# Attention with mean-pooled queries and a two-layer MLP on one core: unsplit float32 for the first five head pairs, and keys that are kept in DRAM

## The chip, the cores and the metric

One core of a Trainium2 chip runs one program. The metric is the device time of one execution in microseconds (us). The kernel before was run three times: median 1096.42 us, from 1094.15 to 1097.43.

## The reference

```python
def _attn_ref(q, k, v):                       # 4 batches, 8 heads, 1152 keys, 64 per head
    q_pool = q.reshape(B, H, S // 2, 2, D).mean(axis=3)
    scores = scale * np.matmul(q_pool, k.transpose(0, 1, 3, 2))
    scores = scores - np.max(scores, axis=-1, keepdims=True)
    attn = np.exp(scores)
    attn = attn / (np.sum(attn, axis=-1, keepdims=True) + 1e-09)
    return np.matmul(attn, v)
def _moe_ref(x, w_in, w_out):                 # x: 2304 x 512, 512 -> 2048 -> 512
    h = x @ w_in
    g = np.maximum(0.01 * h, h)
    return g @ w_out
```

The attention output, with the heads side by side, is x. All inputs are float32, but for w_in and w_out, which are float64 and are converted in the kernel.

## The kernel before, in words

**Split numbers.** Each operand of a large matmul is written as hi + lo. ScalarE (ACT) copies it from PSUM into the type float32r, which gives hi; VectorE (DVE) subtracts that from the original, which gives lo. The keys of a head are stacked in `kk` (hi in one half of the 128 partitions, lo in the other), the queries are doubled in `qq`, so two matmuls per 384 columns (lines 393, 394 and 397, 398) give all four products. In P·V the values hi and lo stand side by side in `vv` as 128 output columns, and the two parts of `et` are streamed through them one after the other (line 477, 18 matmuls per unit); `norm` adds the two halves of the result.

**Units.** A unit is one head of one batch and one group of its 576 pooled query rows: group 0 has 256 rows in 2 tiles, group 1 has 320 rows in 3 tiles. Batches 0, 1 and 2 (`HALF_FIRST`) are passed twice: first group 0 of all eight heads, then group 1 of all eight; batch 3 is passed once, both groups of a head after each other. That makes 64 units: 0 to 7 are group 0 of batch 0, 8 to 15 its group 1, 16 to 31 are batch 1, 32 to 47 batch 2, 48 to 63 batch 3. Heads are taken in pairs (segments `sg`); a pair's keys are loaded, transposed (`k_tr`, line 311, nine transposes), and split (`k_hi`, `k_lo`, line 326) anew in each pass, so batches 0 to 2 do it twice.

**A unit's steps.** `load_q`, `q_sum` (GpSimd, POOL), `q_tr`, `q_hi`, `q_lo` (line 357); for each tile `qk`, `vmax` (line 406, the maximum from PSUM on DVE), `exp` (line 420, ACT); then `rsum` (lines 429, 433: sum and reciprocal on DVE), `r_tr` (line 438: the reciprocals transposed, so that they lie along the columns), `tr` (line 457: 18 or 27 transposes of the exponentials), `e_hi` (ACT) and `e_lo` (line 466, DVE), `pvm` (line 477), `norm` (ACT copy, DVE line 489, POOL line 492), and `x_out` (line 497), which writes a piece of x to DRAM. `tr` of a unit comes after its `r_tr`, by an order constraint.

**The MLP** goes over nine blocks of 256 rows of x: `x_load` (line 571), `l1` (line 593, 192 matmuls of 256 columns per block), `post`, `l2` (lines 615 to 617, 96 matmuls of 512 columns per block). Block 0 needs units 0 to 7, blocks 6, 7 and 8 need batch 3. The 32 weight tiles are converted from float64 along the way (`w_load`, `w_f32`, `w_hi`, `w_lo`: lines 520 to 545, seven passes of 512 columns each over ACT, DVE and POOL).

**Order.** A planner (`Scheduler`) places every step on its engine at build time: of the steps that can start, by the costs that it assumes, it takes the one with the lowest `prio`, which is counted in tiles with offsets (`AHEAD`, `SOONER`, `TR`, `PV`, `WIN`, `WOUT`). Each engine then runs its list in that order. SyncE (SP) issues all DMAs, from one list. The eight PSUM banks are handed out by tags: `s` (one slot of two banks, scores of 768 columns), `s2` (one bank, the other 384), `t` (three banks, all transposes), `o` (P·V), `ml` (one bank, the MLP).

Of the kernel before, what the change touches and what calls it, by code (L numbers as in the profile page):

```python
# [150 lines left out]
def tile_pooled_attention_moe(  # L151
# [52 lines left out]
    NU = len(units)  # L204
    visits = {}
# [54 lines left out]
    stats = [sb.tile([128, 12], F32, name=f"stat{i}") for i in range(3)]  # L260
    xd = [dram.tile([DM, SP], F32, name=f"xd{b}") for b in range(B)]
# [11 lines left out]
    tags["ml"] = [(None, 0, slots("bank", (6,))), (tail, 0, slots("bank", (0,), (1,), (2,), (3,), (4,), (7,)))]  # L273
# [31 lines left out]
    def k_tr(sg, gi, e, i, *heads):  # L305
        for j, x in enumerate(heads):
            kk[2 * sg + j] = new("kk", x)
# [19 lines left out]

    qn, qs, qps, qq = {}, {}, {}, {}
# [16 lines left out]
    def q_tr(u, e, i, s):  # L345
        p, t = QG[units[u][2]]
        qq[u] = new("qq", s)[:, :, :p * t]
# [13 lines left out]
    vn, vv = {}, {}  # L361

# [49 lines left out]
    def exp(u, j, part, e, i=None, s=None):  # L412
# [5 lines left out]
        d = ex[u, j][:n, 2 * CW:] if part else ex[u, j][:n, :2 * CW].rearrange("p (c k) -> p c k", c=2)  # L418
# [40 lines left out]
    def e_hi(u, x, e, i):  # L459
        et[u, x] = new("et", i)  # L460
# [9 lines left out]
    def pvm(u, x, e, i=None):  # L470
# [4 lines left out]
        for a, t in enumerate(kts(u)[x]):  # L475
            for y in range(2):
# [5 lines left out]
    def norm(u, step, e, i):  # L482
# [152 lines left out]

    def trs(*rows):
# [17 lines left out]
    for u in range(NU):  # L654
# [8 lines left out]
        if u == us[0]:  # L663
            if j == 0:
                for part in range(1 if sg else len(KLOAD)):
                    before = ("load_k", sg, part - 1) if part else ("load_k", sg - 1, 0 if sg > 1 else len(KLOAD) - 1) if sg else None
                    step(load_k, sg, part, prio=pr - 4 + 0.01 * part - (0 if sg else 50), **sp(1, 0.59e6 if sg else 0.15e6), order=[before],
                         takes=[("kn", [("k_tr", sg, NCH - 1)])] if part == 0 else [])
                heads = [2 * sg, 2 * sg + 1]
                for gi in range(NCH):  # L670
                    hold = [(f, sg, gi, x) for f in ("k_hi", "k_lo") for x in range(len(KPART[gi]))]
                    need = [0] if sg else [[0], [1, 2], [3]][gi]
                    step(k_tr, sg, gi, prio=pr + 0.1 * gi, eng=trs(128, 128, 128),
                         deps=[("load_k", sg, x) for x in need] + [("k_tr", sg, gi - 1) if gi else ("k_tr", sg - 1, NCH - 1) if sg else None],
                         takes=[("t", hold)] + ([("kk", [("qk", us_of[x][-1], len(tiles_of(us_of[x][-1])) - 1, 1)]) for x in heads] if gi == 0 else []))
# [3 lines left out]
            step(load_v, hd, prio=pr + 2, **sp(1, 0.3e6), order=[("load_v", hd - 1) if hd else None], takes=[("vr", [("v_lo", hd)])])  # L679
            step(v_hi, hd, prio=pr + 5, eng={"ACT": act(576), "DVE": dve(576, 2)}, deps=[("load_v", hd)], order=[("v_hi", hd - 1) if hd else None], takes=[("vv", [("pvm", us[-1], len(kts(us[-1])) - 1)])])  # L680
            step(v_lo, hd, prio=pr + 5, eng={"POOL": gp(576)}, deps=[("v_hi", hd)])
# [24 lines left out]
        step(r_tr, u, prio=p0 - 1, eng=trs(*[x[1] for x in tiles_of(u)]), deps=[("rsum", u, 1)], takes=[("t", [("r_cp", u)])])  # L706
        step(r_cp, u, prio=p0 - 1, eng={"ACT": act(w, True)}, deps=[("r_tr", u)], takes=[("rb", [("norm", u, 2)])])
# [96 lines left out]
```

## Time and profile before

| | us |
|---|---|
| median of three runs | 1096.42 |
| the profiled execution | 1097.69 |
| its span, first to last instruction | 1095.9 |
| PE (TensorE) busy | 997.1 (91%) |
| DVE / ACT / POOL busy | 775.8 / 689.6 / 406.2 |
| 16 DMA engines, mean busy share | 44% |

The span is what the rows of the trace add up to; the profiled execution is 1.8 us longer, and 1.3 us above the median. Busy time of PE overstates its work, since a matmul's record includes its way through the array, while the next one already follows: what a matmul costs in a row of matmuls is the distance between two starts.

### The profile page before, as it was taken

To read this page: it belongs to the slowest core of one execution; us is meant where nothing else is said; L and a number is where in the kernel's file an instruction comes from. 1 tells how busy PE (TensorE), PEld (TensorE's weight loads), DVE (VectorE), ACT (ScalarE), POOL (GpSimd) and SP (SyncE) were. 2 spreads that over 40 slices of the span, in tenths; PEclk is the share of its full clock that TensorE was granted. 3 is DMA by queue.
4 is the path that set the end of the run, shared out by engine and by line. 5 is a ranking of instruction groups with operands and counts; after the bars stand their busy time and mean duration, and the time that the engine had idled before them with its cause. 6 is when DMAs were issued, how large, how long until landed. Compare 5 with 4: busy or idle time off the path is not lost.

```text
span 1095.9 us, 19300 instructions
## 1 busy us (share of the span) xinstructions
PE 997.1 (91%) x6748; PEld 906.3 (83%) x6748; DVE 775.8 (71%) x1625; ACT 689.6 (63%) x1693; POOL 406.2 (37%) x402
## 2 busy tenths in 40 slices
PE   5666788988999989999999999999999999799998
PEld 4555677787898979989899989988999888789896
DVE  7898889997788787777788788776778666411110
ACT  6777877877677666667677667776667665311110
POOL 5666557654233243222434242223222231133220
PEclk8788989999999999999999999999999999899999
DMA  8866546252264353524444433524243130286640
GB/s 263 283 213 214 179 141 232 84 210 90 73 203 143 103 161 100 170 79 150 144 157 134 136 129 116 182 66 162 76 136 105 30 125 25 63 293 231 191 164 29
DMA packets 83953, 158.55 MB, mean 145 GB/s; under 512 B 8592, under 2 KB 44944, under 8 KB 83856
## 3 DMA queue, kind: packets, MB, share of 16 engines
q1 hardware_dynamic: 83856, 157.32, 43.8%
q8 instruction: 53, 0.87, 0.3%
q14 instruction: 44, 0.36, 0.1%
HBM read 139.46 MB, written 17.83 MB: 144 GB/s over the span
## 4 chain that ended last, share of the span: by engine, by line
PE 68%; DVE 18%; issue 5%; DMA 4%; ACT 2%; POOL 2%; SPq 0%; DVEq 0%; POOLq 0%; ACTq 0%
PE banks L593 15%; PE banks L457 11%; PE banks L477 11%; PE banks L615 5%; PE banks L617 5%; PE banks L616 5%; DVE mx L406 5%; PE banks L393 4%; PE banks L394 4%; DVE kk L326 3%; DVE et L466 2%; PE banks L397 2%; PE banks L311 2%; PE banks L398 2%; DVE raw L529 2%
## 5 line engine op out<-in xcount | busy, mean ns | idle before, releaser
L466 DVE TENSOR_TENSOR et<-banks,et 128x320 fp32r<-128x320 f32 (+2 forms) x448 | 233.5, 536 | 70.3 <-ACT et L194 66.8
L194 ACT CAST et<-banks 128x320 fp32r<-128x320 f32 (+2 forms) x448 | 201.2, 470 | 120.5 <-PE banks L477 67.0
L406 DVE TENSOR_REDUCE mx<-banks 128x1 f32<-128x768 f32 (+2 forms) x320 | 234.2, 751 | 60.0 <-PE banks L394 49.9
L420 ACT ACTIVATE e<-banks,mx 128x768 f32<-128x768 f32 (+2 forms) x320 | 238.2, 745 | 56.6 <-DVE mx L410 49.8
L477 PE MATMUL banks<-et,vv 128*128 128x320 f32 (+1 forms) x1152 | 245.9, 323 | 5.8 <-DVE mx L410 4.1
L593 PE MATMUL banks<-xb,ws 128*128 128x256 f32 x1728 | 243.9, 286 | 7.8 <-ACT g L601 2.2
L457 PE MATMUL banks<-ident,e 128*128 128x128 f32 (+2 forms) x1440 | 219.2, 275 | 33.7 <-DVE et L466 14.5
L593 PEld LDWEIGHTS banks<-xb,ws 128*128 128x128 f32 x1728 | 224.2, 190 | 15.5 <-ACT g L601 4.8
L457 PEld LDWEIGHTS banks<-ident,e 128*128 128x128 f32 (+2 forms) x1440 | 174.9, 147 | 61.9 <-DVE et L466 21.6
L477 PEld LDWEIGHTS banks<-et,vv 128*128 128x128 f32 x1152 | 171.0, 194 | 10.8 <-DVE mx L410 5.0
L343 POOL TENSOR_TENSOR qs<-qn 80x256 f32<-80x256 f32 (+1 forms) x128 | 78.5, 633 | 195.8 <-PE banks L351 134.0
L606 POOL TENSOR_TENSOR gg<-g,gg 128x512 fp32r<-128x512 f32 x62 | 80.2, 1294 | 178.4 <-DVE gg L194 146.2
L393 PE MATMUL banks<-kk,qq 128*128 128x384 f32 (+2 forms) x320 | 118.1, 369 | 9.3 <-ACT e L420 9.1
L373 POOL TENSOR_TENSOR vv<-vr,vv 128x576 fp32r<-128x576 f32 x56 | 80.2, 1432 | 97.1 <-DVE vv L194 87.7
L394 PE MATMUL banks<-kk,qq 128*128 128x384 f32 (+2 forms) x320 | 111.4, 348 | 1.0 <-DVE qq L357 1.0
L326 DVE TENSOR_TENSOR kk<-banks,kk 64x384 fp32r<-64x384 f32 (+1 forms) x224 | 98.9, 454 | 14.2 <-ACT kk L194 10.0
L601 ACT ACTIVATE g<-banks 128x512 f32<-128x512 f32 x72 | 43.0, 597 | 102.2 <-PE banks L593 101.5
L615 PE MATMUL banks<-wo,gg 128*128 128x512 f32 x248 | 101.9, 411 | 0.9 <-ACT g L601 0.7
L194 ACT CAST kk<-banks 64x384 fp32r<-64x384 f32 (+1 forms) x224 | 83.9, 392 | 23.6 <-PE banks L311 13.7
L617 PE MATMUL banks<-wo,gg 128*128 128x512 f32 x248 | 97.6, 394 | 0.0
L616 PE MATMUL banks<-wo,gg 128*128 128x512 f32 x248 | 97.4, 393 | 0.0
L492 POOL TENSOR_TENSOR xo<-x,rb 64x256 f32<-64x256 f32 (+1 forms) x64 | 53.1, 829 | 71.4 <-DVE x L489 67.3
(60 smaller groups left out, 1275.1 us busy)
## 6 DMA issues: line engine op xcount, KB each, us to landing
ws<-wd SPq DMA_DIRECT2D x144, 512.0 KB, 4.3
vr<-in_v_dram SPq DMA_DIRECT2D x56, 288.0 KB, 3.4
kn<-in_k_dram SPq DMA_DIRECT2D x27, 576.0 KB, 3.9
raw<-in_moe_w_in_dram SPq DMA_DIRECT2D x16, 512.0 KB, 5.4
wd<-ws SPq DMA_DIRECT2D x16, 512.0 KB, 4.1
raw<-in_moe_w_out_dram SPq DMA_DIRECT2D x16, 512.0 KB, 5.0
qn<-in_q_dram SPq DMA_DIRECT2D x32, 160.0 KB, 2.4
out_dram<-raw SPq DMA_DIRECT2D x18, 256.0 KB, 2.0
```

What stands on the lines that cost most here:

```text
L194: ENG[e].copy(out=out, in_=in_) if e == "ACT" else ENG[e].tensor_copy(out=out, in_=in_)
L393: nc.tensor.matmul(p[:, c], lhsT=hi, rhs=key[:, c * CW:(c + 1) * CW], start=True, stop=False)
L394: nc.tensor.matmul(p[:, c], lhsT=lo, rhs=key[:, c * CW:(c + 1) * CW], start=False, stop=True)
L406: nc.vector.tensor_reduce(out=m[:, part:part + 1], in_=sps[u, j, part], axis=(AX.XY, AX.X)[part], op=ALU.max)
L420: nc.scalar.activation(out=d, in_=sps.pop((u, j, part)), func=AF.Exp, bias=mxs[u, j][:n, 2:3], accum_out=st[u][:n, c:c + 1])
L457: nc.tensor.transpose(p[:, a * w + o:a * w + o + n], ex[u, j][:n, t * 128:(t + 1) * 128], ident[:n, :n])
L466: nc.vector.tensor_tensor(out=et[u, x][:, 1, :w], in0=tps.pop((u, x))[:, :w], in1=f32(et[u, x])[:, 0, :w], op=ALU.subtract)
L477: nc.tensor.matmul(p, lhsT=vv[vis_of[u]][:, korder[vis_of[u] % 2][t], :], rhs=et[u, x][:, y, a * w:(a + 1) * w], start=(t == 0 and y == 0) ...
L593: nc.tensor.matmul(p, lhsT=wst[i, f][:, a, c, :], rhs=xx[i][:, x, c, :], start=(n == 0), stop=(n == 3 * KC - 1))
L615: nc.tensor.matmul(p, lhsT=gh, rhs=wo[f][:, 0], start=(f == hf * FH), stop=False)
L616: nc.tensor.matmul(p, lhsT=gh, rhs=wo[f][:, 1], start=False, stop=False)
L617: nc.tensor.matmul(p, lhsT=gl, rhs=wo[f][:, 0], start=False, stop=(f == hf * FH + FH - 1))
```

## The change

The first five head pairs (`PLAIN = 5`: units 0 to 9) stay in unsplit float32. Their keys are copied once (`k_cp`, ACT or DVE), with one pair's two heads in one `kk` tile; `qk` is three float32 matmuls per tile that contract over 64 partitions (512 + 512 columns from the two halves of the partitions, then 128); `e_hi` is one copy on either engine, with no `e_lo`; `pvm` is nine float32 matmuls of 64 output columns; V is loaded straight into `vv`; `norm_plain` is one DVE multiply. The split keys of the eight pairs of batches 1 and 2 are written to DRAM in the first pass (`k_save`) and read back in the second (`k_back`), which drops their second `k_tr`, `k_hi` and `k_lo`. `r_tr` gets a later priority, loses the order constraint and produces 64 partitions instead of 128. Until the exponential of unit 7's second tile, `s` has two slots (banks 0, 1 and 6, 7), `t` has two banks and `ml` has none. The planner's offsets change.

```diff
+PLAIN = 5
+KEEP = True
+RT = 2.5
+EARLY = 7
-AHEAD = 3.0
-SOONER = 4.0
-TR, SPLIT, PV = 1.5, 1.0, 2.0
+AHEAD = 4.0
+SOONER = 6.0
+TR, SPLIT, PV = 2.0, 1.0, 3.0
-WIN = (-2.0, 0.8)
-WOUT = (20.0, 1.0)
+WIN = (0.0, 1.0)
+WOUT = (16.0, 0.6)
...
+    kept = {sg: first_seg[bh] for sg, bh in enumerate(seg_bh) if KEEP and PLAIN <= first_seg[bh] < sg}
...
-    tags["s"] = [(None, 0, slots("bank", (0, 1)))]
+    early = ("exp", EARLY, 1, 0)
+    tags["s"] = [(None, 0, slots("bank", (0, 1))), (None, early, slots("bank", (6, 7)))]
-    tags["t"] = [(None, 0, slots("bank", (3,), (4,), (7,)))]
+    tags["t"] = [(None, 0, slots("bank", (3,), (4,))), (early, 0, slots("bank", (7,)))]
...
+    def k_cp(sg, gi, e):
+        copy(e, kk[2 * sg][:, gi * CW:(gi + 1) * CW], kps.pop((sg, gi)))
+    def k_save(hd, e):
+        nc.sync.dma_start(out=kd[hd], in_=f32(kk[hd]))
+    def k_back(hd, e, i):
+        kk[hd] = new("kk", i)
+        nc.sync.dma_start(out=f32(kk[hd]), in_=kd[2 * kept[hd // 2] + hd % 2])
...
+        if plain(u):
+            head = units[u][4]
+            p = new(("s", "s2")[part], i)
+            p = sps[u, j, part] = p[:n, :128] if part else p[:n]
+            for c in [2] if part else [0, 1]:
+                half, first, m = ((head, 4 + 4 * head, 1) if part else ((head + c) % 2, (4 + c) * head, 4))
+                nc.tensor.matmul(
+                    p if part else p[:, c], lhsT=qq[u][64 * half:64 * half + 64, 0, o:o + n],
+                    rhs=kk[2 * units[u][3]][64 * half:64 * half + 64, 128 * first:128 * (first + m)], start=True, stop=True,
+                )
+            return
...
-            nc.tensor.transpose(p[:, o:o + n], st[u][:n, 8 + j:9 + j].to_broadcast([n, 128]), ident[:n, :n])
+            nc.tensor.transpose(p[:64, o:o + n], st[u][:n, 8 + j:9 + j].to_broadcast([n, 64]), ident[:n, :n])
...
+            if plain(u):
+                nc.tensor.matmul(
+                    p[0:64], lhsT=vv[vis_of[u]][:, (0, 2, 4, 6, 1, 3, 5, 7, 8)[t], :], rhs=et[u, x][:, 0, a * w:(a + 1) * w],
+                    start=(t == 0), stop=(t == KT - 1),
+                )
+                continue
...
+    def norm_plain(u, e, i):
+        w = width(u)
+        xos[u] = new("xo", i)[:, :w]
+        nc.vector.tensor_tensor(out=xos[u], in0=pv.pop(u)[0:64, :w], in1=rbs.pop(u), op=ALU.mult)
...
+            if sg in kept:
+                step(k_back, hd, prio=pr + 0.1, **sp(1, 0.59e6), deps=[("k_save", 2 * kept[sg] + j)],
+                     order=[("k_back", hd - 1) if j or sg - 1 in kept else ("k_tr", sg - 1, NCH - 1)], takes=[("kk", hold)])
...
-        step(r_tr, u, prio=p0 - 1, eng=trs(*[x[1] for x in tiles_of(u)]), deps=[("rsum", u, 1)], takes=[("t", [("r_cp", u)])])
+        step(r_tr, u, prio=p0 + RT, eng=trs(*[64 for x in tiles_of(u)]), deps=[("rsum", u, 1)], takes=[("t", [("r_cp", u)])])
...
-                 deps=[("exp", u, t, x) for t in range(ntile) for x in range(2)], order=[("r_tr", u)] if x == 0 else [("tr", u, x - 1)], takes=[("t", [("e_lo", u, x)])])
+                 deps=[("exp", u, t, x) for t in range(ntile) for x in range(2)], order=[("tr", u, x - 1)] if x else [("r_tr", u)] if RT < 0 else [], takes=[("t", [("e_hi" if plain(u) else "e_lo", u, x)])])
```

What it moves is seen at three places. The first is the head of VectorE's list (`kk` are keys, `qq` queries, `mx` maxima, `raw` and `ws` weights). Before:

```order
L326 TENSOR_TENSOR kk<-banks,kk 64x384 x2
L357 SCALAR_TENSOR_TENSOR qq<-banks,qq 128x256
L326 TENSOR_TENSOR kk<-banks,kk 64x256
L326 TENSOR_TENSOR kk<-banks,kk 64x128
L326 TENSOR_TENSOR kk<-banks,kk 64x256
L406 TENSOR_REDUCE mx<-banks 128x1 x2
L326 TENSOR_TENSOR kk<-banks,kk 64x128
```

Now:

```order
L453 TENSOR_REDUCE mx<-banks 128x1 x3
L457 TENSOR_REDUCE mx<-mx 128x1
L584 TENSOR_SCALAR raw<-raw 128x512 x2
L588 SCALAR_TENSOR_TENSOR raw<-raw 128x512 x2
L453 TENSOR_REDUCE mx<-banks 128x1
L457 TENSOR_REDUCE mx<-mx 128x1
L200 CAST ws<-raw 128x512
L200 COPY kk<-banks 128x384
```

VectorE starts with the maxima of the first two tiles, where it started with the lo parts of the keys and the queries. The second place is TensorE's list at a split unit of group 1, where the reciprocals are transposed (`stat` holds them). Before:

```order
L397 MATMUL banks<-kk,qq 108x384
L398 MATMUL banks<-kk,qq 108x384
L351 MATMUL banks<-ident,qs 128x128 x2
L438 MATMUL banks<-ident,stat_67 128x108
L438 MATMUL banks<-ident,stat_67 128x106 x2
L457 MATMUL banks<-ident,e 128x108
L457 MATMUL banks<-ident,e 128x106 x2
L393 MATMUL banks<-kk,qq 106x384
```

Now (line 505 transposes the exponentials, 531 is P·V, 437 and 438 are scores, 486 is `r_tr`):

```order
L505 MATMUL banks<-ident,e 128x108
L505 MATMUL banks<-ident,e 128x106 x2
L531 MATMUL banks<-et,vv 128x320 x4
L437 MATMUL banks<-kk,qq 106x384
L438 MATMUL banks<-kk,qq 106x384
L437 MATMUL banks<-kk,qq 106x384
L438 MATMUL banks<-kk,qq 106x384
L486 MATMUL banks<-ident,stat_67 64x108
L486 MATMUL banks<-ident,stat_67 64x106 x2
L531 MATMUL banks<-et,vv 128x320 x2
```

The three small transposes stood ahead of all the unit's other transposes and now stand behind them, among its P·V matmuls. The third place is SyncE's list in the second pass of batch 1, with buffer numbers (`kd` is the DRAM copy of a head, `qn` the queries of one unit, `ws` an MLP weight tile):

```order
L349 DMA kd23_75<-kk_3259 128x1152
L353 DMA kk_3539<-kd17_69 128x1152
L642 DMA ws_3550<-wd11_99 128x1024
L363 DMA qn_3624<-in_q_dram 80x4x128
L398 DMA vr_3647<-in_v_dram 128x576
L642 DMA ws_3657<-wd12_100 128x1024
L556 DMA xd1_85<-xo_3660 64x256
L642 DMA ws_3681<-wd13_101 128x1024
L353 DMA kk_3712<-kd18_70 128x1152
L363 DMA qn_3742<-in_q_dram 80x4x128
```

Where one load of a pair's keys (`kn`) stood for two units, there is now one read-back per unit, next to the load of that unit's queries.

## Rows read from the trace of the kernel before

**Rows 1.** The page: its title line, the PE and DVE slices, and TensorE's granted clock.

```profile
span 1095.9 us, 19300 instructions
...
PE   5666788988999989999999999999999999799998
...
DVE  7898889997788787777788788776778666411110
...
PEclk8788989999999999999999999999999999899999
```

**Rows 2.** The issues of x to DRAM (L497) and of its loads for the MLP (L571).

```profile
L497 SPq DMA_DIRECT2D xd<-xo x64: 446/451/718, 39.4 to 953.3; - x64
L571 SPq DMA_DIRECT2D xb<-xd x48: 319/430/1548, 142.0 to 1023.2; - x48
```

**Rows 3.** Busy time by stretch: its length, PE, PEld, DVE, ACT, POOL, PEclk, DMA share, GB/s.

```profile
0.00:20.00 20.00, 11.19 (x40) 8.69 (x40) 12.48 (x24) 13.39 (x29) 7.31 (x17) 1.00 0.80 252
20.00:141.00 121.00, 81.09 (x462) 69.59 (x462) 109.34 (x207) 91.70 (x213) 76.71 (x71) 0.83 0.66 220
141.00:289.00 148.00, 131.69 (x881) 117.09 (x882) 131.64 (x265) 111.18 (x273) 76.91 (x68) 0.97 0.42 143
289.00:388.00 99.00, 94.67 (x701) 88.58 (x700) 78.63 (x170) 71.77 (x177) 38.76 (x43) 1.00 0.48 153
388.00:520.00 132.00, 127.38 (x898) 117.15 (x897) 101.21 (x224) 91.91 (x236) 39.00 (x40) 1.00 0.39 127
...
953.00:1096.00 143.00, 136.64 (x858) 122.57 (x856) 15.79 (x32) 17.88 (x30) 36.03 (x27) 0.99 0.54 181
```

**Rows 4.** VectorE's groups from 20 to 141 us, those that the change touches.

```profile
L466 DVE TENSOR_TENSOR et<-banks,et 128x512 fp32r<-128x512 f32 x32 | 21.6, 682 | 1.0 <-ACT et L194 0.8
...
L326 DVE TENSOR_TENSOR kk<-banks,kk 64x384 fp32r<-64x384 f32 x16 | 8.9, 554 | 0.4
...
L326 DVE TENSOR_TENSOR kk<-banks,kk 64x256 fp32r<-64x256 f32 x8 | 3.4, 420 | 0.2
L466 DVE TENSOR_TENSOR et<-banks,et 128x256 fp32r<-128x256 f32 x8 | 3.3, 413 | 0.2 <-ACT et L194 0.2
L489 DVE TENSOR_TENSOR x<-banks,t 64x256 f32<-64x256 f32 x8 | 3.3, 409 | 0.2
L194 DVE CAST vv<-vr 128x576 fp32r<-128x576 f32 x4 | 3.0, 745 | 0.7 <-PE banks L477 0.7
L357 DVE SCALAR_TENSOR_TENSOR qq<-banks,qq 128x256 fp32r<-128x256 f32 x6 | 2.5, 414 | 0.0
L326 DVE TENSOR_TENSOR kk<-banks,kk 64x128 fp32r<-64x128 f32 x8 | 2.3, 288 | 0.2
```

**Rows 5.** All groups by form, whole span: the one plain VectorE copy out of PSUM.

```profile
L194 DVE COPY raw<-banks 128x512 f32<-128x512 f32 x1 | 0.7, 691 | 0.3 <-PE banks L617 0.3
```

**Rows 6.** Chain of waits, 285 to 296 us, at full clock: start, us, what.

```profile
286.83 0.18 PE banks L393
...
289.73 0.23 PE banks L617
289.96 1.09 PE banks L457 x10
291.06 0.94 PE banks L477 x8
```

**Rows 7.** Timeline of PE from 22 us, in a stretch at half clock: start, us, line.

```profile
23.27 0.52 PE L394 MATMUL banks<-kk,qq 128*128 128x384 f32 x1
23.59 0.52 PE L393 MATMUL banks<-kk,qq 128*128 128x384 f32 x1
```

**Rows 8.** PE groups by form, whole span: P·V and the transposes of keys.

```profile
L477 PE MATMUL banks<-et,vv 128*128 128x256 f32 x576 | 100.8, 301 | 4.9 <-DVE mx L410 4.1 <-DVE et L466 0.7
...
L311 PE MATMUL banks<-ident,kn 128*128 128x128 f32 x252 | 41.1, 284 | 7.8 <-DMA kn<-in_k_dram 4.4 <-ACT rb L194 2.2 <-DVE kk L326 1.1
```

**Rows 9.** PE's first transposes of reciprocals of group 1: 141 to 289, then 289 to 953 us.

```profile
L438 PE MATMUL banks<-ident,stat 108*128 108x108 f32 x8 | 2.5, 307 | 9.6 <-DVE kk L326 7.7 <-DVE stat L433 1.4 <-DVE qq L357 0.6
...
L438 PE MATMUL banks<-ident,stat 108*128 108x108 f32 x24 | 7.0, 291 | 9.3 <-DVE kk L326 5.4 <-DVE stat L433 3.9
```

**Rows 10.** DMA issues: names, count, KB each, median us to landing.

```profile
kn<-in_k_dram SPq DMA_DIRECT2D x27, 576.0 KB, 3.9
...
wd<-ws SPq DMA_DIRECT2D x16, 512.0 KB, 4.1
```

More of the change, by code (lines that the diff above doesn't have):

```diff
@@ L204, in tile_pooled_attention_moe, with plain @@
     NU = len(units)
+    first_seg = {}
+    for sg, bh in enumerate(seg_bh):
+        first_seg.setdefault(bh, sg)
+    kept = {sg: first_seg[bh] for sg, bh in enumerate(seg_bh) if KEEP and PLAIN <= first_seg[bh] < sg}
+    def plain(u):
+        return units[u][3] < PLAIN
     visits = {}
@@ L260, in tile_pooled_attention_moe @@
     stats = [sb.tile([128, 12], F32, name=f"stat{i}") for i in range(3)]
+    kd = {2 * sg + j: dram.tile([128, S], F32, name=f"kd{2 * sg + j}") for sg in set(kept.values()) for j in range(2)}
     xd = [dram.tile([DM, SP], F32, name=f"xd{b}") for b in range(B)]
@@ L306, in k_tr @@
         for j, x in enumerate(heads):
-            kk[2 * sg + j] = new("kk", x)
+            kk[2 * sg + j] = new("kk", x, F32 if sg < PLAIN else None)
         p = new("t", i)[:, :CW]
@@ L346, in q_tr @@
         p, t = QG[units[u][2]]
-        qq[u] = new("qq", s)[:, :, :p * t]
+        qq[u] = new("qq", s, F32 if plain(u) else None)[:, :, :p * t]
         w = qs.pop(u).rearrange("p t j d -> p t (j d)")
@@ L361, in tile_pooled_attention_moe, with load_vv @@
     vn, vv = {}, {}
+    def load_vv(hd, e, i):
+        b, h = seg_bh[hd // 2]
+        vv[hd] = new("vv", i, F32).rearrange("p t d -> p (t d)")[:, :KT * D].rearrange("p (t d) -> p t d", t=KT)
+        nc.sync.dma_start(out=vv[hd], in_=v[b, h + hd % 2].rearrange("(p t) d -> p t d", t=KT))
     def load_v(hd, e, i):
@@ L459, in e_hi @@
     def e_hi(u, x, e, i):
-        et[u, x] = new("et", i)
+        et[u, x] = new("et", i, F32 if plain(u) else None)
         w = width(u) * len(kts(u)[x])
@@ L634, in mm, with mm4 @@
         return {"PE": sum(0.0035 + 0.000445 * max(c, 240) for c in cols)}
+    def mm4(*cols):
+        return {"PE": sum(0.01 + 0.00182 * c for c in cols)}
     def trs(*rows):
@@ L663, in tile_pooled_attention_moe @@
         if u == us[0]:
-            if j == 0:
+            hold = [("qk", us[-1], len(tiles_of(us[-1])) - 1, 1)] + ([("k_save", hd)] if sg in kept.values() else [])
+            if sg in kept:
+                step(k_back, hd, prio=pr + 0.1, **sp(1, 0.59e6), deps=[("k_save", 2 * kept[sg] + j)],
+                     order=[("k_back", hd - 1) if j or sg - 1 in kept else ("k_tr", sg - 1, NCH - 1)], takes=[("kk", hold)])
+            elif j == 0:
                 for part in range(1 if sg else len(KLOAD)):
-                    before = ("load_k", sg, part - 1) if part else ("load_k", sg - 1, 0 if sg > 1 else len(KLOAD) - 1) if sg else None
+                    last = max([x for x in range(sg) if x not in kept], default=None)
+                    before = ("load_k", sg, part - 1) if part else ("load_k", last, 0 if last else len(KLOAD) - 1) if sg else None
                     step(load_k, sg, part, prio=pr - 4 + 0.01 * part - (0 if sg else 50), **sp(1, 0.59e6 if sg else 0.15e6), order=[before],
@@ L685, in tile_pooled_attention_moe @@
         step(q_tr, u, prio=pr + 1, eng=trs(*[qp] * qt), deps=[("q_sum", u), ("q_tr", prev) if u else None],
-             takes=[("t", [("q_lo", u)]), ("qq", [("qk", u, ntile - 1, 1)])])
+             takes=[("t", [("q_hi" if plain(u) else "q_lo", u)]), ("qq", [("qk", u, ntile - 1, 1)])])
         step(q_hi, u, prio=pr + 1, eng={"ACT": act(w, True)}, deps=[("q_tr", u)])
-        step(q_lo, u, prio=pr + 1, eng={"DVE": dve(w, psum=True)}, deps=[("q_hi", u)])
+        if not plain(u):
+            step(q_lo, u, prio=pr + 1, eng={"DVE": dve(w, psum=True)}, deps=[("q_hi", u)])
         for t in range(ntile):
@@ L705, in tile_pooled_attention_moe @@
         step(rsum, u, 1, prio=p0, eng={"DVE": 0.17}, deps=[("rsum", u, 0)])
-        step(r_tr, u, prio=p0 - 1, eng=trs(*[x[1] for x in tiles_of(u)]), deps=[("rsum", u, 1)], takes=[("t", [("r_cp", u)])])
-        step(r_cp, u, prio=p0 - 1, eng={"ACT": act(w, True)}, deps=[("r_tr", u)], takes=[("rb", [("norm", u, 2)])])
+        step(r_tr, u, prio=p0 + RT, eng=trs(*[64 for x in tiles_of(u)]), deps=[("rsum", u, 1)], takes=[("t", [("r_cp", u)])])
+        step(r_cp, u, prio=p0 - 1, eng={"ACT": act(w, True)}, deps=[("r_tr", u)], takes=[("rb", [("norm_plain", u) if plain(u) else ("norm", u, 2)])])
         nx = len(kts(u))
```

58 lines of the change are left out of this document (44 added, 14 removed).

## The prediction

> **What bounds the kernel now.** The first view is the page's slices [rows 1]. Look at PE and DVE slice by slice: in the first five (to 137 us) TensorE is at 5 to 7 tenths and its granted clock mostly below full, while VectorE is at 7 to 9; from the tenth slice on VectorE is below TensorE. So there are two kernels in one. The places where they meet come from the DMA issues [rows 2]: the first piece of x is read back for the MLP at 142.0 us, when units 0 to 7 have written theirs, and the last unit writes at 953.3 us. Up to 142 us TensorE has nothing but attention; behind it the MLP's matmuls fill its gaps; behind 953 us only blocks 6 to 8 are left, which need batch 3.
>
> The busy times of these stretches [rows 3] say what limits each. From 20 to 141 us VectorE is busy for 109.3 of 121 us (90%), TensorE for 81.1 at a mean clock of 0.83: VectorE sets the end. From 141 to 289 us VectorE (131.6 of 148) and TensorE (131.7) are level at 89%. From 289 us on TensorE is busy for 94.7 of 99 and 127.4 of 132 us (96%): it sets the end, and VectorE's 77 to 79% has room. The last 143 us hold 576 matmuls of 256 columns and 288 of 512, which at 0.1175 and 0.23 us [rows 6] are 134 us of work: nothing here touches them.
>
> What a matmul costs is read from the chain at full clock, where the starts follow each other [rows 6]: 0.109 us for a transpose of 128 columns (1.09 for ten), 0.1175 for 256 columns of the split type (0.94 for eight), 0.175 for 384, 0.23 for 512. At half clock 384 columns take 0.32 [rows 7].
>
> **Stage 1 (to 142 us): VectorE is relieved, TensorE is loaded.** What leaves VectorE between 20 and 141 us is nearly all of its eight touched groups [rows 4]: the lo parts of the exponentials (21.6 + 3.3 us), of the keys (8.9 + 3.4 + 2.3), of the queries (2.5), V's hi parts (3.0) and the first add of `norm` (3.3): 48.3 us. What comes, by the new list: 11 copies of 512 columns at 0.69 (the one such copy that the trace has [rows 5]), 4 of 256 and 6 of 384 at 0.41 and 0.55 (same sizes, rows 4), 8 multiplies of 256 at 0.41: 15.8 us. ScalarE takes the other copies, and loses more than it gets. Maxima and exponentials keep their columns (1024 + 128 for 768 + 384). So VectorE has 32.5 us less; with the same 11.7 us of idle time its stretch would end at 108.5 us.
>
> TensorE, per unit at full clock, before: scores 12 x 0.174 = 2.1, P·V 18 x 0.1175 = 2.1, 26.5 transposes of 0.109 = 2.9: 7.1 us, 57 for the eight. Now P·V is 9 float32 matmuls of 256 columns. No row shows a float32 matmul that is not a transpose. Lower bound: a transpose, float32 too, has 0.85 ns per column against 0.46 for the split type, so twice the split price, 0.235 us, and P·V would cost no more than before. Upper bound: the four products of halves that the split kernel computes, at its price, 4 x 0.1175 = 0.47 us. I take the upper one, since a full product needs all four and a transpose multiplies by ones and zeros: +17 us for the eight units. Scores: two pieces of 512 columns at 0.92 and one of 128 at 0.23 per tile. The two pieces use different halves of the partitions; no row shows two matmuls at once. Bounds: side by side 1.15 us per tile, one after the other 2.07, against 1.04 before: +1.7 or +16.5 us. So TensorE's work becomes 75 or 90 us. I take 90, what the trace knows to happen; at 92% busy and full clock this ends at 20 + 98 = 118 us. Full clock, because the gaps in which it fell (waits of several us for VectorE and ScalarE) are those that go. Were it 75, VectorE's 108.5 would decide: 118 is 24 us less than 142.
>
> The Trainium skill ("TensorEngine Tiling (Array Packing)", Key Properties) says that tiles of different row halves execute in parallel; by it TensorE would have the 75 us, and the whole would come 9 us lower than my sum. No row here shows it, and my sum goes without.
>
> The second slot for scores costs `t` one of three banks and `ml` its bank, which is not used before 142 us. Transposes then have two banks for 8.5 uses per unit of some 12 us; each is held for about 1.2 us: hidden by that. DMA is busy for 0.66 of 121 us, 80 us [rows 3]; in 98 us that still fits, at 0.8.
>
> **The reciprocals last.** Their first transpose of a group-1 unit idles TensorE for 9.6 us in all between 141 and 289 us, and for 9.3 us between 289 and 953 us [rows 9], nearly all on VectorE. In the new list transposes and P·V stand ahead, which need nothing from `rsum`. What is late next is the multiplication at the end, off the path. Bounds: all 18.9 us, or nothing, where VectorE is as late with the split of the exponentials. I take 5 of the 9.6, since VectorE is level with TensorE there, and 6 of the 9.3.
>
> **Keys kept.** 72 of the 252 transposes of keys [rows 8] go, 72 x 0.109 = 7.8 us of TensorE, in the stretches that it bounds. The hi and lo parts of eight pairs go too, off the path: VectorE has room there. Against it stand 16 writes and 16 reads of 576 KB for 8 loads of 576 KB, 14 MB more; the DMA engines are at 0.39 to 0.48 [rows 3] and go to about 0.5. A write waits for the lo parts and holds up SyncE's list behind it until then; the lists show one per unit or so between loads that are issued early. A read-back stands next to the query load of its own unit, and lands in about 4 us, as the nearest rows do (3.9 and 4.1 [rows 10]); the queries need two sums, a transpose and a split after that. I cost both at nothing; that cover gone, a read would cost up to its 4 us, 16 times.
>
> **Units 8 and 9.** P·V +5 us of TensorE (18 more 320-column passes of 0.147 x 2), VectorE about even: two of the weight conversions move in from stage 1. I take 3 us of cost.
>
> **Sum.** -24 - 5 - 6 - 7.8 + 3 = -40 us. The profiled execution took 1097.7 us (span 1095.9), so 1058; it lies 1.3 us above the median, so I predict **1056**. What stage 1 gains is kept, since every later stretch is bounded by work that only starts earlier.
>
> **Rivals.** *More is gained*: stage 1 at VectorE's 108.5 us, all of rows 9. -9.5 - 8 gives 1038. For it: the pairs overlap. Against: three engines with 75 to 80 us each wait for each other more than one full one does.
>
> *Changing the shape of the array costs.* Scores now use half of the rows, P·V and the reciprocals half of the columns, all else the whole: 238 changes in the list, 100 of them in stage 1. If each empties the array, it costs at most what a record is longer than the distance of two starts, 301 - 117.5 = 0.18 us [rows 6, 8]: 18 us in stage 1 and 25 behind it, 1099 in all, 1078 at half that. Against: the trace has only whole-array shapes, which follow without a gap. The skill's same page and section states that a change of mode drains TensorE; that is this rival, and the reason that I give it 0.22.
>
> *TensorE sets stage 1 at a low clock*: slower. Its place is units 0 to 7, its price 90 us of work divided by the granted clock. At the 0.83 of before it ends at 20 + 109/0.92 = 138 us, 1076 in all. It turns to slower where stage 1 lasts beyond 142 + 16 = 158 us, a mean clock under 0.71; at 0.65 it is 171 us, 1109 in all. For it: the clock of that stretch fell again and again. Against: TensorE was idle then, and now has a third to a half more to do.
>
> *The read-backs come late*, so that the kept keys don't save but cost: 16 x 4 = 64 us, 1120, and no gain from 2.6 us each on. Against: the place in SyncE's list.
>
> **How the numbers follow.** Chances: the forecast (1046 to 1068) 0.45, more 0.15, shape changes 0.22, low clock 0.11 (half of it slower), late reads 0.07. Faster by over 0.3% (3.3 us, what a measurement of this kernel can tell) holds the first two, most of the shape changes, half of the clock: 0.80. Within: 0.07. Slower: 0.13. The range 1036 to 1091 leaves out the far ends of the last three and little below.
>
> **What would show it.** Right: the first x load (142.0 us before) at 112 to 124 us; VectorE's busy time up to there near 90 us, TensorE's clock near 1; float32 P·V matmuls 0.47 us apart; no wait of the reciprocals' transposes for VectorE; the stretch from 953 us on still 143. Wrong: P·V more than 0.5 us apart at full clock, gaps at every change of shape, or TensorE waiting for `kk` from `kd`. If the first x load comes before 125 us and the total is still above 1075, the gain was given back later, and the step "kept, since every later stretch is bounded by work" is what fails.

## The result, and the profile after

Measured against the kernel before on the same chip: **1054.51 us** (median of four, 1051.20 to 1055.03) against 1095.29 us, a ratio of 0.962, 95% interval 0.959 to 0.965. Forecast were 1056 us and 1036 to 1091. The total is right to 2 us, and that is luck: the three stretches that it was summed from came out at -32, +15 and -25 us where -24, -2 and -14 were forecast, and the errors cancel. So the experiments ask what each part is worth.

The page of the changed kernel, the slices of PE and DVE and the granted clock, against [rows 1]:

```profile
span 1053.2 us, 18894 instructions
...
PE   6999788899999999999999999999999999999998
...
DVE  4777889888888667777877676786877766411110
...
PEclk8999799999999999999999999999999999999999
```

TensorE is at 9 tenths from the second to the fourth slice, VectorE starts at 4 and 7: they have changed places in the first stage. The fifth slice of PE and of the clock stays at 7, as before; it is now a dip behind a full stage. The issues of x and of its loads, against [rows 2]:

```profile
L556 SPq DMA_DIRECT2D xd<-xo x64: 451/452/1286, 31.8 to 913.5; - x64
L630 SPq DMA_DIRECT2D xb<-xd x48: 319/430/1217, 112.2 to 980.8; - x48
```

The first load of x comes at 112.2 us instead of 142.0. The busy times by stretch, cut at the outputs of the same units as [rows 3] (columns as there):

```profile
0.00:20.00 20.00, 11.07 (x35) 6.08 (x35) 6.76 (x14) 10.54 (x21) 7.43 (x18) 0.85 0.81 264
20.00:112.00 92.00, 89.72 (x463) 49.66 (x461) 68.42 (x138) 64.32 (x147) 51.19 (x49) 0.99 0.80 260
112.00:271.00 159.00, 142.91 (x901) 117.00 (x902) 135.56 (x269) 114.44 (x279) 79.36 (x71) 0.95 0.48 164
271.00:353.00 82.00, 78.04 (x581) 74.05 (x581) 67.46 (x140) 58.28 (x140) 35.06 (x39) 1.00 0.60 197
353.00:489.00 136.00, 132.22 (x940) 122.96 (x939) 99.32 (x221) 90.15 (x230) 41.52 (x43) 1.00 0.47 155
...
914.00:1053.00 139.00, 132.32 (x833) 118.36 (x831) 15.56 (x32) 17.29 (x29) 35.71 (x26) 1.00 0.56 184
```

In the first stage TensorE is busy for 89.7 of 92 us at a clock of 0.99, and VectorE for 68.4. The second stretch is longer than before, 159 against 148 us. Behind it the first pass of batch 1 is 17 us shorter (82 against 99) and its second pass, the one with the read-backs, 4 us longer (136 against 132): the planner has put 60 fewer of `l1`'s matmuls into the one and 36 more into the other. The issue times of units 7 and 15, used from here on, are 141.5 and 289.1 us before, 109.0 and 271.3 after.

### The profile page after: what moved, and what is told of

It is laid out like the page before. It is cut to its first block, busy times and chain, and to the rows that moved or that the text cites. A ratio compares the mean times of both kernels' runs of the same rounds, so it can differ in the third digit from the quotient of the medians.

```text
span 1053.2 us, 18894 instructions
## 1 busy us (share of the span) xinstructions
PE 998.6 (95%) x6676; PEld 870.8 (83%) x6676; DVE 701.8 (67%) x1479; ACT 642.0 (61%) x1558; POOL 382.8 (36%) x382
## 4 chain that ended last, share of the span: by engine, by line
PE 81%; DVE 10%; ACT 3%; issue 3%; DMA 2%; POOL 1%; SPq 1%; DVEq 0%; ACTq 0%; POOLq 0%
PE banks L652 15%; PE banks L505 13%; PE banks L531 11%; PE banks L674 6%; PE banks L676 6%; PE banks L675 6%; PE banks L525 4%; PE banks L437 4%; PE banks L438 4%; DVE mx L453 3%; PE banks L428 3%; PE banks L441 2%; PE banks L442 2%; PE banks L328 2%; PE banks L486 2%
## 5 line engine op out<-in xcount | busy, mean ns | idle before, releaser
L453 DVE TENSOR_REDUCE mx<-banks 106x1 f32<-106x768 f32 (+4 forms) x320 | 235.3, 753 | 84.8 <-PE banks L438 45.7
L468 ACT ACTIVATE e<-banks,mx 106x768 f32<-106x768 f32 (+4 forms) x320 | 237.5, 744 | 54.2 <-DVE mx L457 47.4
L200 ACT CAST et<-banks 128x320 fp32r<-128x320 f32 (+2 forms) x390 | 171.6, 466 | 101.2 <-PE banks L531 47.9
L514 DVE TENSOR_TENSOR et<-banks,et 128x320 fp32r<-128x320 f32 (+2 forms) x390 | 199.1, 528 | 50.5 <-ACT et L200 48.4
L531 PE MATMUL banks<-et,vv 128*128 128x320 f32 (+1 forms) x972 | 207.3, 320 | 3.2 <-DVE et L514 2.1
L531 PEld LDWEIGHTS banks<-et,vv 128*128 128x128 f32 x972 | 142.6, 189 | 6.9 <-DVE et L514 2.9
L437 PE MATMUL banks<-kk,qq 128*106 128x384 f32 (+2 forms) x276 | 96.5, 350 | 2.0 <-ACT e L468 2.0
L438 PE MATMUL banks<-kk,qq 128*106 128x384 f32 (+2 forms) x276 | 93.0, 337 | 0.0
L546 POOL TENSOR_TENSOR xo<-x,rb 64x320 f32<-64x320 f32 (+1 forms) x54 | 44.1, 816 | 71.6 <-DVE x L543 62.3
L468 ACT ACTIVATION_READ_ACCUMULATOR e<-banks,mx 128x1 f32 (+2 forms) x320 | 63.9, 200 | 0.0
L200 DVE CAST gg<-g 128x512 fp32r<-128x512 f32 x55 | 25.4, 462 | 47.8 <-ACT g L660 47.1
```

The costliest lines, as they stand in the source:

```text
L200: ENG[e].copy(out=out, in_=in_) if e == "ACT" else ENG[e].tensor_copy(out=out, in_=in_)
L437: nc.tensor.matmul(p[:, c], lhsT=hi, rhs=key[:, c * CW:(c + 1) * CW], start=True, stop=False)
L438: nc.tensor.matmul(p[:, c], lhsT=lo, rhs=key[:, c * CW:(c + 1) * CW], start=False, stop=True)
L453: nc.vector.tensor_reduce(out=m[:, part:part + 1], in_=sps[u, j, part], axis=(AX.XY, AX.X)[part], op=ALU.max)
L468: nc.scalar.activation(out=d, in_=sps.pop((u, j, part)), func=AF.Exp, bias=mxs[u, j][:n, 2:3], accum_out=st[u][:n, c:c + 1])
L514: nc.vector.tensor_tensor(out=et[u, x][:, 1, :w], in0=tps.pop((u, x))[:, :w], in1=f32(et[u, x])[:, 0, :w], op=ALU.subtract)
```

## The experiments

All edits are to the changed kernel. "Unit 7" and "unit 15" are the issue times of their outputs in the profiled run, in us; the ratio is to the kernel before, run beside it.

| run | median us | ratio, 95% interval | unit 7 | unit 15 | span |
|---|---|---|---|---|---|
| changed kernel | 1054.51 | 0.962 (0.959 to 0.965) | 109.0 | 271.3 | 1053.2 |
| e1_rtr128 | 1054.61 | 0.959 (0.956 to 0.963) | 109.5 | 269.8 | 1054.6 |
| e2_pv128 | 1048.46 | 0.955 (0.952 to 0.959) | 103.4 | 264.0 | 1046.6 |
| e3_onehalf | 1083.62 | 0.986 (0.983 to 0.989) | 131.6 | 296.7 | 1079.2 |
| e4_rfirst | 1088.02 | 0.991 (0.988 to 0.994) | 124.5 | 283.7 | 1085.5 |
| e5_nokeep | 1069.85 | 0.974 (0.971 to 0.977) | 110.9 | 273.1 | 1068.5 |
| e6_plain0 | 1094.19 | 0.997 (0.996 to 0.999) | 148.4 | 309.6 | 1093.6 |
| e7_onescore | 1053.72 | 0.960 (0.958 to 0.963) | 112.0 | 270.0 | 1050.4 |
| e9_weights | 1075.91 | 0.981 (0.978 to 0.984) | 138.2 | 289.6 | 1072.4 |
| f1_pv128_one | 1048.78 | 0.955 (0.952 to 0.957) | 113.1 | 270.0 | 1049.6 |
| f2_plain4 | 1066.73 | 0.970 (0.967 to 0.972) | 123.3 | 280.5 | 1068.0 |
| f3_plain6 | 1061.58 | 0.966 (0.964 to 0.968) | 110.9 | 276.5 | 1061.1 |
| f4_wout | 1048.64 | 0.954 (0.951 to 0.956) | 103.5 | 263.6 | 1043.7 |

### What a float32 matmul and a change of shape cost

First the trace itself. TensorE in the first stage of the changed kernel, at full clock (start, time from the first start to the last end, line; a float32 matmul that is no transpose leaves two records, so x4 is two of them):

```profile
22.96 1.09 PE L505 MATMUL banks<-ident,e 128*128 128x128 f32 x8
23.98 1.08 PE L525 MATMUL banks<-et,vv 128*64 128x256 f32 x4
...
27.59 1.08 PE L525 MATMUL banks<-et,vv 128*64 128x256 f32 x4
28.59 0.41 PE L486 MATMUL banks<-ident,stat 128*64 128x128 f32 x2
28.93 1.51 PE L525 MATMUL banks<-et,vv 128*64 128x256 f32 x6
...
50.99 2.37 PE L525 MATMUL banks<-et,vv 128*64 128x256 f32 x10
53.30 0.44 PE L378 MATMUL banks<-ident,qs 128*128 128x128 f32 x2
...
53.99 1.13 PE L428 MATMUL banks<-kk,qq 64*128 64x512 f32 x4
55.05 0.66 PE L505 MATMUL banks<-ident,e 128*128 128x128 f32 x4
55.64 0.49 PE L428 MATMUL banks<-kk,qq 64*128 64x128 f32 x2
56.05 0.66 PE L505 MATMUL banks<-ident,e 128*128 128x128 f32 x4
...
58.28 1.08 PE L525 MATMUL banks<-et,vv 128*64 128x256 f32 x4
59.29 0.66 PE L505 MATMUL banks<-ident,e 128*128 128x128 f32 x4
59.88 1.08 PE L525 MATMUL banks<-et,vv 128*64 128x256 f32 x4
```

Read the distances of the starts. Five float32 P·V matmuls take 2.31 us (50.99 to 53.30), 0.46 each. Two score pieces of 512 columns take 1.06 us together (53.99 to 55.05), where one alone would need 4 x 0.23 = 0.92: they run side by side. Four transposes ahead of a float32 P·V matmul or of scores take 0.59 us instead of 4 x 0.109 = 0.44 [rows 6].

**e3_onehalf** takes the side-by-side away:

```diff
-half, first, m = (... if part else ((head + c) % 2, (4 + c) * head, 4))
+half, first, m = (... if part else (head, (4 + c) * head, 4))
```

> The changed kernel, with both 512-column score matmuls of a tile taken from the same half of the partitions, so half of the score columns belong to other keys than they should. Theory (the two halves of the array ran side by side, 1.06 us for the pair): the pair takes 1.84 to 2.0 us, the first stage ends 11 to 15 us later than 112 us, and the time is 1066 to 1072 us. Rival (they never ran side by side): no change, 1054.5 within 2 us.

```profile
55.72 1.98 PE L428 MATMUL banks<-kk,qq 64*128 64x512 f32 x4
57.63 0.55 PE L505 MATMUL banks<-ident,e 128*128 128x128 f32 x3
```

The pair takes 1.91 us (55.72 to 57.63), 0.85 more. The first theory stands; its price was too low: unit 7's output comes 22.6 us later, and 16 pairs of 0.85 us are 13.6. Much of the rest is the start, where this run's matmuls took twice their time for longer:

```profile
31.88 1.97 PE L505 MATMUL banks<-ident,e 128*128 128x128 f32 x8
33.78 1.91 PE L525 MATMUL banks<-et,vv 128*64 128x256 f32 x4
```

The same eight transposes take 1.90 us here (31.88 to 33.78) and 1.02 in the changed kernel (22.96 to 23.98 above). When the P·V matmuls behind them end, e3 is 10.6 us late after only four pairs, which are worth 3.4; the other twelve pairs add 12.0.

**e1_rtr128 and e2_pv128** ask which changes of shape cost. e1 gives the transposed reciprocals their 128 columns back, e2 makes each float32 P·V matmul 128 columns wide (an extra load fills the columns behind the last tile):

```diff
-nc.tensor.transpose(p[:64, o:o + n], st[u][:n, 8 + j:9 + j].to_broadcast([n, 64]), ident[:n, :n])
+nc.tensor.transpose(p[:, o:o + n], st[u][:n, 8 + j:9 + j].to_broadcast([n, 128]), ident[:n, :n])
...
-p[0:64], lhsT=vv[vis_of[u]][:, (0, 2, 4, 6, 1, 3, 5, 7, 8)[t], :], rhs=...
+p, lhsT=vv[vis_of[u]][:, D * (0, 2, 4, 6, 1, 3, 5, 7, 8)[t]:][:, :2 * D], rhs=...
```

> The changed kernel, with the transposed reciprocals brought back to 128 partitions; the order of all lists stays. Theory (only float32 products and half-row scores pay for a change of shape; in the changed kernel's trace a transpose of reciprocals follows a split matmul at its normal distance): 1054.5 us, within 2 us. Rival (every change of the array's shape empties it, 112 such changes here at up to 0.18 us): 1035 to 1048 us.

> The changed kernel, with 128 columns of V per float32 P·V matmul instead of 64 (the upper 64 outputs are not used; one small load of V more per head). Theory (the 0.15 us between the last transpose and the first float32 P·V matmul belong to the float32 operand, not to the shape): the distance stays at 0.15 us over the nominal one, and the time is 1054.5, within 3 us. Rival (it is the half-column shape): the distance falls by 0.1 to 0.2 us at some 25 places of the first stage, and the time by 3 to 5 us.

e1 is as fast as the changed kernel: 112 changes less behind the first stage are worth nothing. e2 is 6 us faster in three of its four executions (1048.4 us; the fourth took 1054.8), nearly all of it ahead of unit 7 (103.4 against 109.0). Its TensorE timeline at the same kinds of place:

```profile
27.53 0.38 PE L488 MATMUL banks<-ident,stat 128*64 128x128 f32 x2
27.75 1.46 PE L527 MATMUL banks<-et,vv 128*128 128x256 f32 x6
...
56.46 0.60 PE L507 MATMUL banks<-ident,e 128*128 128x128 f32 x4
56.90 1.03 PE L527 MATMUL banks<-et,vv 128*128 128x256 f32 x4
57.76 0.38 PE L507 MATMUL banks<-ident,e 128*128 128x128 f32 x2
```

The four transposes take 0.44 us now (56.46 to 56.90), and the two P·V matmuls 0.86 (56.90 to 57.76) instead of 1.01 (58.28 to 59.29 above). So 0.15 us go at each of the two changes. Up to unit 7's output 21 stretches of P·V begin behind a transpose and 25 end ahead of one; 46 x 0.15 = 6.9 us is the estimate from these distances, and unit 7 gains 5.6. The theory written for e2, that float32 operands cost and not the shape, falls: with 128 columns the cost is gone. For the transposed reciprocals the rival falls.

The number of columns alone does not decide it, though. In the changed kernel the transposed reciprocals have the same 64 columns as the P·V matmuls around them, and two still take 0.34 us (28.59 to 28.93). In e2 they are the only ones of the three with 64 columns, and take 0.22 (27.53 to 27.75). So what costs is the way from 64-column P·V matmuls to a transpose, of either width, and back; why is open. The Trainium skill's rule that a change of tiling mode drains TensorE ("TensorEngine Tiling (Array Packing)", Key Properties) agrees with the P·V stretches, at 0.15 us each way; the traces show columns and not modes, so the reciprocals say nothing for or against it. The Trainium skill's rule in the same section that different tiles can work in parallel agrees with the pairs of scores on two halves of the rows: 1.06 us, against 1.91 in e3.

### What each part is worth

**e6_plain0** splits all pairs (`PLAIN = 0`, with the same keys kept), **e4_rfirst** puts the transposed reciprocals back (`RT = -1.0`), **e9_weights** the old due times (`WIN`, `WOUT`), **e5_nokeep** sets `KEEP = False`, **e7_onescore** gives `s` one slot, `t` three banks and `ml` its own bank throughout.

> The changed kernel with every head pair split, the same keys kept. Theory (VectorE set the end of the first stage, and the float32 products are what relieved it): the first x load at 125 to 140 us instead of 112, VectorE busy for about 90% up to there, 1070 to 1085 us in all. Rival (the reciprocals' place and the second score tile did it): below 118 us, and within 8 us of 1054.5.

```profile
20.00:138.00 118.00, 78.98 (x416) 67.98 (x414) 104.71 (x191) 82.15 (x188) 65.03 (x63) 0.75 0.62 199
```

Without the float32 pairs the first stage is the old one again: VectorE busy for 104.7 of 118 us (89%), TensorE for 79 at a clock of 0.75, unit 7 at 148.4 and the first x load at 148.9, later than in the kernel before. The expected time was 9 to 24 us too good: the kernel is 0.3% faster than the kernel before, where the whole change makes 3.8%.

> The changed kernel, with the transposed reciprocals at their old priority and ahead of the unit's other transposes. Theory (the waits of TensorE for the reciprocals, 18.9 us behind 141 us in the kernel before, were worth about 11 us): 1061 to 1070 us, with 10 to 20 us of TensorE waiting at this line again. Rival (where they wait, the split of the exponentials is as late): within 3 us of 1054.5.

TensorE's idle time ahead of the first transpose of a unit's reciprocals (group 0, then group 1), in e4 and then in the changed kernel:

```profile
L486 PE MATMUL banks<-ident,stat 128*64 128x128 f32 x64 | 12.9, 284 | 5.6 <-DVE stat L481 5.2 <-DVE kk L343 0.2 <-ACT e L468 0.2
...
L486 PE MATMUL banks<-ident,stat 108*64 108x108 f32 x32 | 8.7, 272 | 16.4 <-DVE stat L481 12.6 <-DVE kk L343 3.7
```

```profile
L486 PE MATMUL banks<-ident,stat 128*64 128x128 f32 x64 | 12.3, 273 | 0.2 <-DVE et L514 0.2
...
L486 PE MATMUL banks<-ident,stat 108*64 108x108 f32 x32 | 8.4, 262 | 1.3 <-DVE mx L457 0.6 <-DVE et L514 0.6
```

The waits come back, 22.0 us against 1.5, as expected. The loss is larger, 0.029 of the time before or 31 us, where 11 were expected: 15 ahead of unit 7 and 20 behind unit 15, less 3 between. Ahead of unit 7 only 3.4 us of idle time stand at these transposes; 7.8 more stand at other places, and from 96 to 110 us the granted clock is at its lower level:

```profile
96.00:110.00 14.00, 10.46 (x30) 4.74 (x32) 12.01 (x21) 9.03 (x23) 11.96 (x9) 0.51 0.86 285
```

How the one brings about the other is not shown. As a whole the place of these two or three small transposes per unit is the second largest part.

> The changed kernel with the old due times of the weight conversions. Theory (the stretch from 109 to 271 us lost 14 us against before, because the second half of the conversions was pulled into it): that stretch is 8 to 12 us shorter, and the first one a little longer; in all 1048 to 1056 us. Rival (what it lost comes from the float32 units 8 and 9 and the gap at half clock when the second score slot ends): the stretch keeps 155 us or more.

```profile
20.00:112.00 92.00, 76.63 (x348) 41.13 (x347) 63.21 (x124) 60.34 (x133) 54.45 (x50) 0.87 0.82 271
```

The second stretch does become 11 us shorter (151.4 against 162.3), and the first one 29 us longer. Before unit 7's output 25 of the 32 weight tiles are put together in float32, against 17 in the changed kernel and 19 in the kernel before; from 20 to 112 us no engine is full (TensorE 77 of 92 us, VectorE 63), TensorE's wait ahead of one query transpose alone is 6.4 us, and the clock falls to 0.87. The old due times cost 21 us here. That they suit a stage bounded by VectorE and not one bounded by TensorE is argued: they were not varied in the kernel before.

> The changed kernel without the kept keys: the second pass loads, transposes and splits the keys again. Theory (72 transposes of 0.109 us on the engine that sets the end, the DMAs hidden): 1060 to 1066 us, the difference between 270 and 711 us, nothing ahead of that. Rival (writes and reads cost as much as they save): 1054.5 within 3 us. Second rival (the lo parts of the keys on VectorE mattered too): over 1068 us.

Busy time from unit 15's output to that of unit 47, the last of batch 2, without and then with the kept keys:

```profile
273.15:721.60 448.45, 431.29 (x3092) 401.79 (x3091) 352.40 (x764) 323.78 (x808) 153.28 (x161) 1.00 0.43 134
```

```profile
271.30:710.60 439.30, 421.82 (x3028) 392.67 (x3027) 333.87 (x716) 300.94 (x748) 153.58 (x161) 1.00 0.51 166
```

In these batches the theory holds. TensorE is busy for 96% either way and sets the end; with the kept keys it has 9.5 us less to do, and the stretch is 9.2 us shorter, of which the keys' transposes are 7.8; without them nine more matmuls of the MLP stand there too, 2 us. VectorE and ScalarE have 18.5 and 22.8 us less to do, at 76 to 79% and 69 to 72%. The whole time, 0.012 or 13 us, is over the theory's range and in that of the second rival. But the rest of the difference lies where no key is kept: 1.9 us ahead of unit 15 and 5.9 in batch 3, less 1.6 at the end. What makes it is not shown; the planner places all steps anew. The DMA engines go from 0.43 to 0.51, about as forecast. The read-backs land in 4.1 us, as loads of keys do; the writes take 5.2:

```profile
kd<-kk SPq DMA_DIRECT2D x16, 576.0 KB, 5.2
kk<-kd SPq DMA_DIRECT2D x16, 576.0 KB, 4.1
```

> The changed kernel with one score slot and three banks for transposes from the start. Theory (TensorE is full in the first stage, a second slot only takes out the few waits for the exponential): first x load 2 to 6 us later, 1057 to 1061 us. Rival (the second slot carries the stage): 10 us or more later. Rival (the lost transpose bank costs as much): no change.

The second score slot is worth nothing: 3 us ahead of unit 7, given back by unit 15 (270.0 against 271.3), and a ratio within the interval. The third case of the expectation comes nearest.

Where the parts are lost is seen when each run is cut at units 7 and 15 (us longer than the changed kernel, one profiled execution each):

| undone | to unit 7 | unit 7 to 15 | behind unit 15 |
|---|---|---|---|
| float32 pairs (e6) | 39.4 | -1.1 | 2.1 |
| place of the reciprocals (e4) | 15.4 | -3.0 | 19.8 |
| due times (e9) | 29.2 | -10.9 | 0.9 |
| kept keys (e5) | 1.9 | 0.0 | 13.4 |
| everything (kernel before) | 32.4 | -14.6 | 24.9 |

The float32 pairs are worth the first stage and nothing else: behind unit 15, e6 keeps 22.8 of the 24.9 us. It loses them again ahead of unit 15, where it is slower than the kernel before in both stretches.

### The second stretch, and a better version

The chain of waits where the second stretch begins (start, us, what):

```profile
109.67 1.06 PE banks L428 x4
...
110.83 1.42 DVE mx L453 x2
...
112.28 0.56 DVE kk L343
...
113.39 0.57 DVE kk L343
...
114.09 0.77 PE banks L378 x4
114.86 2.00 PE banks L428 x4
...
116.95 1.42 DVE mx L453 x2
...
118.66 0.70 ACT e L468
```

Here the score slots fall from two to one, and the first split pair's lo parts stand on VectorE, so TensorE waits for maxima, lo parts and exponentials in turn. At 114.86 us a pair of score pieces takes 2.00 us instead of 1.06: the granted clock is at its lower level, 1.2 GHz, from 113 to 127 us. The last runs ask what else the stretch pays for, on top of e2's edit: f1 adds e7's, f2 and f3 have four and six float32 pairs in f1's kernel, f4 adds `WOUT = (16.0, 1.0)` to e2.

> The changed kernel with 128 columns of V, and the second half of the weight conversions due over 16 tiles instead of 10, from the same start. Theory (the crowding of conversions behind 109 us costs that stretch 5 to 10 us): the stretch to unit 15's output falls from 161 us to 151 to 156, the first stage stays at 103 to 105 us. Rival (its loss is the TensorE work and the low clock after the gap at its start): 158 us or more.

> The changed kernel with both parts that were free or better alone: 128 columns of V per float32 P·V matmul, and one score slot with three transpose banks throughout. Theory (the gains add up, since the one is TensorE time in the first stage and the other bank traffic): ratio to the kernel before 0.952 to 0.957, faster than the changed kernel's 0.962. Rival (with TensorE relieved, the single score slot becomes the bound): 0.960 or more.

> The kernel of the run before this one, with four float32 pairs instead of five: group 1 of batch 0 is split throughout. Theory (the stretch behind the first stage is bounded by VectorE and TensorE about equally, so the fifth pair is worth little): within 0.003 of that run's ratio. Rival (VectorE bounds that stretch): 0.004 to 0.01 slower.

> The same with six float32 pairs. Theory (as above): within 0.003. Rival (VectorE bounds the stretch from 109 to 271 us): 0.003 to 0.008 faster.

f4 leaves the stretch at 160.0 us, so its theory is not borne out; but the test is weak, since the same 15 conversions stay in the stretch as in e2 and the last weight tile is put together at 197 us instead of 186. In e9, with eight of them fewer in the stretch, it took 151. f1 is as fast as e2 and no faster: its ratio is in the range of the theory by e2's part alone, and unit 7 comes at 113.1 us. f2 and f3 are both slower than f1, by 0.015 and 0.011, on opposite sides: f2 loses 10 us ahead of unit 7, though units 0 to 7 do the same work in it, f3 loses 9 us in the second stretch. Neither theory had that; a planner that gets another list places all of it anew.

Units 8 and 9 are hardly what lengthens the stretch. It is no shorter where they are split: 157.3 us in f2 against 156.8 in f1, 161.2 in e6 against 162.3. What shortens it is fewer conversions in it (e9, by 10.9 us, for 29 ahead of it) and a single score slot from the start (e7, by 4.3).

**e2_pv128, f1_pv128_one and f4_wout** are the fastest: 0.954 to 0.955 of the time before, with intervals from 0.951 to 0.959. They can't be told apart; the interval of the changed kernel begins at 0.959.

## Why the prediction was right, and where its steps were not

| term of the sum | predicted us | measured us |
|---|---|---|
| start to unit 7's output, from 141.5 | -24 | -32.4 |
| unit 7 to unit 15, from 147.6 | -5 + 3 | +14.6 |
| unit 15 to the end, from 806.8 | -6 - 7.8 | -24.9 |
| sum, from a span of 1095.9 | -40 | -42.7 |

The first term was priced by the first x load, which moved by 29.8 us.

- **What bounds the kernel**: right. VectorE set the first stage, the float32 pairs move it to TensorE, and e6 shows that nothing of the first stage's gain is there without them. The gain behind unit 15 does not need them.
- **VectorE's 32.5 us less** was too little: it is busy for 75 us up to the first x load (6.8 + 68.4 to 112 us), where near 90 was named as a sign. Besides two conversions fewer, the passes that stay are shorter, as this one (up to unit 7, before and now) shows; why is open:

```profile
L529 DVE SCALAR_TENSOR_TENSOR raw<-raw 128x512 uint32<-128x512 uint32 x17 | 15.5, 910 | 0.1
```

```profile
L588 DVE SCALAR_TENSOR_TENSOR raw<-raw 128x512 uint32<-128x512 uint32 x15 | 10.7, 715 | 0.2
```

- **Float32 P·V, upper bound 0.47 us**: right. Five that follow each other take 0.46 us each, and 0.43 without the 0.15 us for the change. The argument, four products of halves, is what the Trainium skill states as four passes ("FP8 and Floating Point Precision", TensorE Precision Notes); the lower bound by the transposes was far off.
- **Scores "I take 90, what the trace knows to happen"**: the step was wrong and its number right. The pieces run side by side (1.06 us per pair), which makes 75 us of work. What the sum had at nothing brings it back near the 89.7 us that TensorE is busy: 0.15 us at each way from P·V to a transpose or back, as much for each run of transposes between two pieces of scores, and 0.41 us for the 128-column piece (55.64 to 56.05) whose own columns need 0.23. So the error of the one step was paid by another.
- **"At 92% busy"**: it was 97.5%, at a clock of 0.99 as forecast. That is the 6 us by which the stage beat its term.
- **The reciprocals, -11 us**: the mechanism was right, since the waits are gone (1.3 us ahead of group 1, from 18.9). The size was a third of the 31 us that undoing it costs in the changed kernel. The step that failed was to price it by the idle time at these transposes alone: in e4 that is 22 us, and most of the loss ahead of unit 7 is not idle time there. What it would bring to the kernel before alone was not measured.
- **Keys, -7.8 us**: right in its place, where the two batches with kept keys are 9.2 us shorter. The whole run pays 13 without them; the rest lies in stretches without kept keys and is not explained.
- **Units 8 and 9, "VectorE about even"**: the worst step in size. The stretch lost 14.6 us where 2 were to be gained. The two conversions did move in as forecast (17 against 19 ahead of unit 7), and the two units are hardly the cause: e6, with none in float32, loses 13.5 us there against the kernel before. The term priced the work that moves and not the plan around it. e7 puts 4.3 us on the place where the score slots fall from two to one, with its gaps and 14 us at the lower clock; what the rest comes from, the planner's new offsets among it, stays open.
- **"The last 143 us: nothing here touches them"**: they are 2.9 us shorter (139.7 against 142.6).
- **The due times of the conversions** were not a term at all, apart from "two of the weight conversions move in". They carry 21 us.
- **Rivals**: the change of shape was there, in the first stage, with 6 us for P·V, and cost nothing in the 112 changes behind it; the low clock showed up behind the stage and not in it; the read-backs were hidden, as nothing in the trace waited for one.

## What to carry to other kernels

Parts that are undone one at a time cost 38, 31, 21 and 13 us here, 103 together, of a gain of 41; ahead of unit 7 alone they cost 86 of a gain of 32. Several parts hold up the same stage, and none has a price of its own. So when work moves from the full engine to an idle one, look in the same step for what makes the idle one wait: the place of the reciprocals was priced at 11 us from the old kernel's idle time and cost 31 in the new one, and the due times, worth 21, were not priced at all. And between float32 products, let the matmuls keep the full width of the array where that is free.

## What was not expected of the hardware

A float32 P·V matmul with 64 output columns costs 0.15 us at the change from a transpose and 0.15 us back, 0.30 us in each alternation, and nothing of it with 128 columns. It pays next to transposes of 64 columns too, so the number of columns alone does not decide it. Transposes with 64 output columns, between split matmuls, cost nothing measurable in 112 changes (ratio 0.959 with 128 columns against 0.962). Two float32 matmuls of 512 columns on different halves of the rows took 1.06 us, on the same half 1.91 us. And a float32 matmul that is no transpose leaves two records each in the trace, so 90 P·V matmuls count as 180.
